# One fused attention and MLP kernel, the same operations in another order table

## The chip, the cores and the metric

The kernel runs on one core of one Trainium2 chip. The metric is the device time of one execution in microseconds (us), as the median of three runs. Five engines work side by side, each through a queue of its own, in order: TensorE (PE in the profile, PEld its weight loads), VectorE (DVE), ScalarE (ACT), GpSimd (POOL) and SyncE (SP). The last two also issue the DMAs: POOL the loads that cast from float32 to bfloat16, SP the stores and the DMA transposes.

## What is computed

Attention over a window of 128 keys and 4 sink keys, for 4 batches of 8 heads, 768 positions and 64 features; its output, 3072 rows of 512, goes through two matrix products with a squared ReLU between them.

```
scores = q @ k^T / sqrt(64);  keep = (pos_k < 4) | (0 <= pos_q - pos_k < 128)
a = softmax(where(keep, scores, -1e9));  x = a @ v            # 4 x 8 x 768 x 64
h = x.reshape(3072, 512) @ w_in                                # 512 x 2048
g = relu(h) ** 2
out = g @ w_out                                                # 2048 x 512, float32
```

## The kernel before

The work is cut into 996 operations, each one or a few instructions on one engine. For every batch: load q, k and v; bring q and k into the layout with the features on the partitions (by transposes on TensorE and copies out of PSUM for batches 0 and 1, lines 508, 193 and 195; by DMA transposes from SP, line 462, for batches 2 and 3); scores into `ps` (L614), the exponential on ScalarE into `expm` (L635); the mask either on VectorE (L647, one instruction for a tile) or on GpSimd (L219, two instructions for a tile); the product with v into `po` (L683); the division by the sum into `xn_sb` (L699, L700); the turn of `xn_sb` into `xT` (L732 on TensorE for batches 0 and 1, DMA transposes L714 for 2 and 3); the scores of the sink keys are `pk` (L573). Layer 1 is `pm` (L764 for batch 0, L892 later), its ReLU `r` (L776 and L967 on ScalarE, L778 and L969 on VectorE), its square `gT_sb` (L785 and L915 on ScalarE, L787 and L917 on VectorE). Layer 2 is `py` (L1239, L1100), gathered into `osb` by copies and additions and stored by L1282. From batch 1 on layer 1, and everywhere layer 2, is a fast product with seven instead of eight partial products; the sums that it needs are `wi`, `wt`, `xs` and `sg` on VectorE (L811, L1031, L1213). The layer-2 products of one batch and the layer-1 products of the next stand between the attention pieces, so that TensorE has work while the other engines prepare its operands.

Nothing in the program decides the order at run time: the table ORDER does, a list of the 996 operations. A letter behind a number picks the engine where more than one can do it (`a` ScalarE, `d` VectorE, `g` GpSimd; without one, the first of its list), and a number behind a plus sign picks which of two pools of PSUM banks gives the room. Each engine's instructions stand in its queue in that order:

```
for word in words:
    word, *chosen = word.split("+")
    n = int(word.rstrip("pdag"))
    o = self.ops[n]
    o.engine = names[word[-1]] if word[-1] in names else next(iter(o.engines))
    for s in o.takes:
        if len(s.pools) > 1:
            s.pool = s.pools[int(chosen.pop(0))]
        s.room = free[s.pool].pop(0)
    self.idle = DUMMIES.get(n, 0)
    o.run(o.engine)
```

PSUM is held in four rooms (two pools of two). An operation that takes a room waits until those that read its last content are done. DUMMIES names small matmuls in front of early operations, all among the first 86, that keep TensorE busy while it waits for the first loads.

Of the kernel before, what the change touches and what calls it, by code (L numbers as in the profile page):

```python
# [20 lines left out]
ORDER = """  # L21
994 0 1 2 7 8 9 10 11 12 13 14 15 16 17 18 995+0 3 5 19 20 21 6 79 22 23 24 25 55d 56d 57+0 58 59 60a 83+0 85 103+1
105 26 27 28 62d 61d 63+1 64 67d 68d 65a 69+0 70 71 72 66a 84+1 73a 74a 75+1 76 78 91+0 86 77a 93 80 113+1 87+0 92+1
89 94 95+0 97 115 88 90 96 98 114+1 99+0 101 117 100 104+0 102 4 29 106 30 107 81+1 31 82 156+0 109+1 116 118 162+0
108d 32 111 157 112 119+1 168+0 121 120 110 123+1 122 125 174+1 163 126 335 169 124a 171+0 131+0 128+1 33 208 34 164
133 170a 175 35 36 37 172 38 132 39 40 158 130a 129a 144+1 146 137+0 176 136+0 147d 145+1 138 140 139d 177+0 278 134+0
148 159+1 135 149d 141d 142+0 279 143 173a 41 178 150+1 282+0 42 151 179a 152+0 43 153a 280 160 154 44 165+0 155a 45
274 189+1 166 180+1 275 276 284 161a 127 285 190d 277 281 283 181 337 286 287 46 192+1 289 196+0 193 200+0 194 197
167a 47 195a 201 297 336 288 48 202 338 183+0 198a 199a 203a 212+0+0 49 290 182 292 184d 215 294 230+0+1 291 299 50
293 298 191 213 231 186+1 204+0 233 295 185 187d 51 52 300 206a 301+0 251+1 303 248+0 205 188a 207a 232d 249a 304 253  # L30
252a 339 316 305d 296 302 219+1+0 216 317 308 53 318 209 306 307d 220 54 222 214 210+0 250a 319 309 234 448 237+0+1
310 311 211 235+0 238 217+0 240 218 236 223 340 466 239d 320+0 449 312 241d 221 450 322 256+0+0 451 259 257 313 452
453 323 454 455 314 341 321 456 242+0 244+0 457 324 458 224+1 327 459 325 460 461 243 471 225 326 226+0 254+1 246 245a
329 228 330 229a 247a 227 331 315 347+1 343 363+1 342 349 469 345 328 332 365 348 364 344 346 255 351 350 333 367
263+1+1 462 366 353 369d 352 479 354 260d 264 368 370 355d 379+0 470 467 266 358 356 468 395+0 258 359 463 371 372
357a 374 360d 361 381 265 373a 380 376 267d 375 474 383 261+0 382 362a 377 397 396 268+0 477 384 262 385 399 386 270+0
475 398 269 387d 272 273 378a 400 473 401 464 478 465 402 271a 489+0+0 390 411 492 490 388 392 403d 391 334 406 404
407 482+0+0 412 393 432+0 483 433 389 476 434 416+1 472 413 394 408 409 436 414 405 417 418 435 534+0 410a 438 420 692
419 536 437 530 422 439 415 421 693 423 532 440 537 485 443 441 491 424 694 427 533 538 444 695 442a 429 696 697 493
531 445 425 539 494+0 428 446 426a 535 495 480+0 540 430 698 447a 498+1+0 481 699 484 486 544 700 499 543 487+0 549  # L40
501 431 488 568 545 713 572+0 505+0+0 569 574 500d 546 541 508 506 542 573 521+0+0 547 710 714 701 579 522 570 575 576
514+1+0 509d 571 496 702 577 703 524 715 578 507 510+0 548 515 523d 582 580 550 723 497 581 583 502 517 585 553+0 551
503+0 511 704 711 516 554 584 587 588 592+0 589 504 594 525 526+0 705 590 518d 555 527 593 717 556 557 591 519+0 712
716 596 520 558 559d 598 552 749+0+0 706 707 595 722 560 561 563 512 750 752 597 599 513 600 562 742+0+0 753d 565d 528
564 603 743 601 751 602 566 604 745 586 726+0+0 529 720 605d 721 608+0 727 609 606 610 660+1 661 662 611 729 624 644+0
718 663 626 612 730 719 724+0 613 625 567 614 725 615 754+0 616 607 728 664 665 645 617 666 646 755 667 618a 648 647
668 619 744 620 649 627 650d 651 731+0 746 669 621 671 672 708 622 676+0 670a 677 673 732 652 674 747+0 623 678 655
653 679 680 656 681 675a 748 657 658 628+1 629 682 630 659 733+1+0 683 774 632 631 734 778+0 684 654a 775 634 685 735
633 779 635 686a 780 636 776 687 688 736 777 709 756 781 689d 690 758+0+1 759 637 782 761 639 640 638a 737 738+0 783
641d 739 642 691a 785 765+0+0 762d 784 760 643 797+0 768 766 793 787 757 799 794 788 769 789 763+0 795 740 767d 790d  # L50
741 791 764 798 786 831 800 801 836+1 837 834 802 832 792 838d 852+0 833 854d 853 840 804 796 855 856 803 839 806 858d
770+0 771 807 857 812 835 813 859 842 808 841 843 772 805 814 810 816+1 860 773 863 861 817 865 844d 864 847 845 809
823 866 818d 846a 868 848 867a 872+0 869 849 874 871 920+0 862 819 850 820 922 873 904+1 870 815 921 905 875 906d 876
877 923 851a 924 821 936 822d 878 879 907 925 811 926 908 880 825 883 827 937 927 881 826 938 882 828 910 885 824 829
884 909 886 888+1 911 928d 889 887 940+0 890 892 942 891 929 893 939 931 894d 932 912 915 930a 895 933 896 934 943 913
916 897 899 914a 944 900 945 935 917 830 946 901 898 941 959+0 902 918 949 947 919a 903 955 957 950 951 956 953 948
961 960 974 962 966 952d 976 978+1 963 975 958 979 964 981+1 965d 954 980 968 967 977 982 983d 970 969 985 984 986 989
972 987 971 988 990 973 993 992 991
"""
DUMMIES = {  # L60
    995: 29, 58: 8, 63: 10, 64: 4, 83: 3, 91: 3, 97: 3,
# [1345 lines left out]
```

## Time and profile before

| what | value |
|---|---|
| median of three runs | 210.26 us (210.16 to 212.4) |
| the profiled execution, its own time | 209.92 us |
| its span, first to last instruction | 208.1 us |
| granted TensorE clock | 1.000 |
| TensorE busy | 198.7 us, 95% of the span |
| VectorE busy | 175.4 us, 84% |
| ScalarE busy | 140.0 us, 67% |
| GpSimd busy | 94.0 us, 45% |
| moved by DMA | 26.12 MB |

The span leaves out 1.82 us of the execution's own time, which lie before the first and behind the last instruction. Matmuls overlap, so that a matmul's duration in the profile is longer than the distance from it to the next; eight matmuls of 256 columns with their weight loads advance TensorE by 0.87 us.

### The profile page before, as it was taken

What the parts mean: (1) busy time and instruction counts of PE and PEld (TensorE: products, weight loads), DVE (VectorE), ACT (ScalarE), POOL (GpSimd) and SP (SyncE); (2) the same over time, 40 slices, a digit from 0 to 9 for tenths busy, and PEclk for the clock granted to TensorE, in tenths of its full rate; (3) what the DMA queues carried; (4) which work ended last, traced back from release to release, by engine and by line L of the source; (5) the groups of instructions that cost most, each with busy time, mean ns of one, the idle gap of its engine ahead of it and who ended that gap; (6) DMA issues with size and microseconds to landing.
All of it is one profiled execution on the core that took longest, in us unless ns stands there. A gap on an engine that the chain in (4) does not pass through costs nothing.

```text
span 208.1 us, 6073 instructions
## 1 busy us (share of the span) xinstructions
PE 198.7 (95%) x2524; PEld 178.7 (86%) x2524; DVE 175.4 (84%) x343; ACT 140.0 (67%) x218; POOL 94.0 (45%) x134
## 2 busy tenths in 40 slices
PE   7779989999999999999999999999999999999993
PEld 7548878998888889889878989998889999999892
DVE  5844647988998899999997988999999998999753
ACT  2686679865895579999977459789892176475010
POOL 7999983597289907319629937100230000000000
PEclk9999999999999999999999999999999999999999
DMA  5999999999999999999999998902022230110205
GB/s 169 278 187 206 174 197 215 166 150 142 158 68 146 147 198 154 166 142 82 143 133 214 110 149 161 186 3 50 3 50 104 30 126 3 41 60 3 101 3 202
DMA packets 93995, 26.12 MB, mean 125 GB/s; under 512 B 86800, under 2 KB 91408, under 8 KB 93968
## 3 DMA queue, kind: packets, MB, share of 16 engines
q0 software_dynamic: 69248, 12.59, 87.1%
q1 hardware_dynamic: 24536, 13.01, 28.7%
q8 instruction: 20, 0.33, 0.6%
q10 hardware_dynamic: 184, 0.14, 0.2%
q14 instruction: 7, 0.06, 0.1%
HBM read 27.30 MB, written 6.29 MB: 161 GB/s over the span
## 4 chain that ended last, share of the span: by engine, by line
PE 70%; DMA 13%; POOL 5%; ACT 4%; DVE 3%; SPq 2%; issue 1%; ACTq 0%; DVEq 0%; POOLq 0%
PE py L1239 31%; PE pm L892 23%; DMA w_out_sb<-in_moe_w_out_dram 6%; PE po L683 5%; PE ps L614 5%; DMA qn<-in_q_dram 4%; DMA qr<-in_q_dram 3%; PE pm L764 2%; POOL expm L219 2%; PE py L1100 2%; SPq L352 2%; ACT expm L635 1%; PE pt L508 1%; ACT gT_sb L915 1%; POOL qn L373 1%
## 5 line engine op out<-in xcount | busy, mean ns | idle before, releaser
L635 ACT ACTIVATE expm<-ps 128x1024 bf16<-128x1024 f32 (+1 forms) x48 | 43.8, 956 | 4.3 <-PE ps L614 3.9
L219 POOL TENSOR_SCALAR_AFFINE_SELECT expm<-expm 128x512 bf16<-128x512 bf16 x30 | 20.9, 726 | 42.2 <-ACT expm L635 33.6
L942 DVE CUSTOM_DVE_ANT_0 r<-pm,t 128x512 bf16<-128x512 f32 x54 | 36.1, 684 | 2.3 <-ACT t L193 1.4
L1239 PEld LDWEIGHTS <-gT_sb 128*128 128x128 bf16 x352 | 33.0, 98 | 4.6 <-issue 1.1
L892 PEld LDWEIGHTS <-w_in_sb 128*128 128x128 bf16 x384 | 32.7, 114 | 1.0 <-issue 0.5
L193 ACT ACTIVATE t<-pm 128x512 f32<-128x512 f32 x42 | 24.9, 599 | 12.3 <-PE pm L892 11.1
L193 ACT ACTIVATE osb<-py 128x256 f32<-128x256 f32 x36 | 13.6, 384 | 26.1 <-PE py L1239 23.7
L1239 PEld LDWEIGHTS <-sg 128*128 128x128 bf16 x264 | 24.9, 98 | 3.4 <-issue 0.8
L892 PEld LDWEIGHTS <-wi 128*128 128x128 bf16 x288 | 24.8, 114 | 0.8 <-issue 0.5
L1239 PE MATMUL py<-wt,sg 128*128 128x256 bf16 x176 | 22.8, 273 | 0.0
L1239 PE MATMUL py<-w_out_sb,gT_sb 128*128 128x256 bf16 x176 | 22.7, 273 | 0.0
L1239 PE MATMUL py<-wt,gT_sb 128*128 128x256 bf16 x176 | 22.7, 273 | 0.0
L764 PE MATMUL pm<-xT,w_in_sb 128*128 128x256 bf16 x192 | 22.5, 273 | 0.1
L915 ACT ACTIVATE gT_sb<-r 128x1024 bf16<-128x1024 bf16 x21 | 22.1, 1058 | 0.7 <-DVE r L942 0.7
L892 PE MATMUL pm<-xs,w_in_sb 128*128 128x256 bf16 (+1 forms) x192 | 21.3, 246 | 0.0
L892 PE MATMUL pm<-xs,wi 128*128 128x256 bf16 (+1 forms) x192 | 21.2, 246 | 0.0
L764 PEld LDWEIGHTS <-w_in_sb 128*128 128x128 bf16 x192 | 20.6, 114 | 0.6 <-issue 0.2
L683 PE MATMUL po<-v,expm 128*128 128x65 bf16 x352 | 18.0, 193 | 0.4 <-ACT expm L635 0.3
L700 DVE TENSOR_TENSOR xn_sb<-po,rc 128x512 bf16<-128x512 f32 (+1 forms) x28 | 17.2, 615 | 1.0
L683 PEld LDWEIGHTS <-expm 128*128 128x128 bf16 x352 | 16.8, 97 | 1.4 <-issue 0.6
L614 PE MATMUL ps<-qkT 64*128 64x128 bf16 (+1 forms) x256 | 14.5, 238 | 1.4 <-ACT qkT L193 1.1
L1253 DVE TENSOR_TENSOR osb<-py,osb 128x256 f32<-128x256 f32 x33 | 13.3, 418 | 2.8 <-PE py L1239 1.9
(107 smaller groups left out, 372.1 us busy)
## 6 DMA issues: line engine op xcount, KB each, us to landing
out_dram<-osb SPq DMA_DIRECT2D x11, 512.0 KB, 3.1
v<-in_v_dram POOLq DMA_DIRECT2D x24, 128.0 KB, 7.0
qn<-in_k_dram POOLq DMA_DIRECT2D x20, 128.0 KB, 6.6
qn<-in_q_dram POOLq DMA_DIRECT2D x20, 128.0 KB, 6.9
w_in_sb<-in_moe_w_in_dram POOLq DMA_DIRECT2D x4, 512.0 KB, 10.1
w_out_sb<-in_moe_w_out_dram POOLq DMA_DIRECT2D x4, 512.0 KB, 9.8
qr<-in_k_dram SPq DMA_DIRECT2D x4, 256.0 KB, 5.3
qr<-in_q_dram SPq DMA_DIRECT2D x4, 256.0 KB, 4.8
```

The lines of the kernel that those rows point to most:

```text
L193: return nc.scalar.activation(out=dst, in_=src, func=AF.Copy)
L219: nc.gpsimd.affine_select(out=e_tile, in_=e_tile, compare_op=ALU.is_ge, fill=fill, base=i - 1, pattern=[[0, n], [1 if i else -1, 128]], ch ...
L614: nc.tensor.matmul(ps[:, h2, o:o + w], lhsT=qkT_sb[r, m, 1, c, :], rhs=qkT_sb[r, m, 0, qb:qb + w // 128, :], start=(i == 0 and not biased) ...
L635: nc.scalar.activation(out=x[:, :, o:512], in_=bank_t["s", b, s, m][:, :, o:512], func=AF.Exp, scale=scale)
L683: touch(("po", b, s, m0), e, nc.tensor.matmul(pv[:, i, h2, :], lhsT=lhsT, rhs=rhs, start=(n_ == 0), stop=(n_ == len(mms) - 1)), j)
L700: touch(("po", b, s, m0), e, nc.vector.tensor_tensor(out=xn_sb[:, 2 * s:2 * s + 2, 128 * (m0 + j0):128 * (m0 + j0 + nj)].rearrange("p i (j ...
L764: nc.tensor.matmul(pm[:, i, :], lhsT=w_in_sb[:, fb // 4, kb, fb % 4:512:4], rhs=xT[:, c0 // 256:(c0 + cw) // 256, kb, :], start=(kb == 0), ...
L892: touch(tag, e, nc.tensor.matmul(y[:, bk, i, :], lhsT=weights(name, f0 + i, a), rhs=rhs[:, a, :], start=fresh and i == 0 and a == 0, stop= ...
L915: nc.scalar.activation(out=d, in_=x, func=AF.Square)
L942: touch(tag, e, nc.vector._custom_dve(TENSOR_ADD_SAT, out=d.rearrange("p n c -> p (n c)"), in0=T["y"][:, 1].rearrange("p n c -> p (n c)"), ...
L1239: touch((b, u), e, nc.tensor.matmul(region(name), lhsT=x[:, i, :], rhs=w_[:, i, :], start=first and i == 0, stop=i == HB - 1, skip_group_c ...
L1253: ins = nc.vector.tensor_tensor(out=d, in0=region(of), in1=d, op=ALU.add)
```

## The change

ORDER is replaced behind its first 86 entries. The operations, their number, the data that they move and DUMMIES stay. What changes is the order on every queue, the engine of 64 pieces that ScalarE or VectorE can do and of 11 masks that VectorE or GpSimd can do, and the choice of some PSUM rooms.

```
 105 26 27 28 62d 61d 63+1 64 67d 68d 65a 69+0 70 71 72 66a 84+1 73a 74a 75+1 76 78 91+0 86 77a 93 80 113+1 87+0 92+1
-89 94 95+0 97 115 88 90 96 98 114+1 99+0 101 117 100 104+0 102 4 29 106 30 107 81+1 31 82 156+0 109+1 116 118 162+0
-108d 32 111 157 112 119+1 168+0 121 120 110 123+1 122 125 174+1 163 126 335 169 124a 171+0 131+0 128+1 33 208 34 164
...
+89 94 95+0 97 115 88 90 96 98 114+1 99+0 101 117 100 104+0 102 4 29 106 81+1 107 156+0 82 157d 158 109+1 116 162+1
+119+0 118 108d 163 121 111 30 110 112 168+0 120 31 122 32 123+1 124a 125 33 208 174+1 126 171+0 164a 175 131+0 169d
...
```

Three places, as the engines' queues read before and now.

GpSimd, the loads of batches 0 and 1 (`qn` and `v` are loads of q, k and v, `w_out_sb` the second weight matrix, `expm` the masks of batch 0, `mask` a constant tile that batch 1 reads); a minus is what stood there before, a plus what stands there now:

```order
 L373 DMA qn<-in_q_dram 128x8x64
-L219 AFFINE_SELECT expm<-expm 128x4x128 x2
+L219 AFFINE_SELECT expm<-expm 128x4x128 x6
 L373 DMA qn<-in_q_dram 128x8x64
-L382 DMA v_181<-in_v_dram 128x8x64
-L219 AFFINE_SELECT expm<-expm 128x4x128 x4
-L382 DMA v_181<-in_v_dram 128x8x64
+L382 DMA v_181<-in_v_dram 128x8x64 x2
 L317 DMA w_out_sb<-in_moe_w_out_dram 128x2048
 L555 TENSOR_TENSOR vs_175<-vs_in,head_rows 32x130 x4
-L317 DMA w_out_sb<-in_moe_w_out_dram 128x2048 x3
```

Two masks now stand ahead of one load of q and one of v. Further on, the three instructions that write `mask` have moved from behind a load of batch 1 to between the second and the third load of `w_out_sb`.

VectorE at the same time, before:

```order
L195 COPY xT_184<-px 128x512 x2
L647 TENSOR_TENSOR expm<-expm,tri 128x1024
L699 RECIPROCAL rc<-po 128x4
L700 TENSOR_TENSOR xn_sb<-po,rc 128x2x128
L699 RECIPROCAL rc<-po 128x4
```

and now:

```order
L195 COPY xT_184<-px 128x512 x2
L778 TENSOR_SCALAR r<-pm 128x1024
L787 TENSOR_TENSOR gT_sb<-r 128x4x256
L647 TENSOR_TENSOR expm<-expm,tri 128x1024
L699 RECIPROCAL rc<-po 128x4
L700 TENSOR_TENSOR xn_sb<-po,rc 128x2x128
```

A ReLU, which ScalarE did before, and its square stand ahead of VectorE's own mask; on TensorE the product that reads this mask has gone behind the two that read GpSimd's.

SP, from the DMA transposes of batch 2's attention output (`xT_184`) to those of batch 3's q and k (`qkT_180`), before:

```order
L714 DMA_TRANSPOSE xT_184<-xn_sb 128x4x128 x3
L1282 DMA out_dram<-osb 128x1024
L714 DMA_TRANSPOSE xT_184<-xn_sb 128x4x128
L462 DMA_TRANSPOSE qkT_180<-qn 128x4x128 x4
L1282 DMA out_dram<-osb 128x2x512
L714 DMA_TRANSPOSE xT_185<-xn_sb 128x4x128 x4
```

and now:

```order
L714 DMA_TRANSPOSE xT_184<-xn_sb 128x4x128 x4
L462 DMA_TRANSPOSE qkT_180<-qn 128x4x128 x4
L1282 DMA out_dram<-osb 128x2x512
L1282 DMA out_dram<-osb 128x1024
L714 DMA_TRANSPOSE xT_185<-xn_sb 128x4x128 x4
```

A store has moved behind the four transposes of q and k. Within the four the first of k (operation 718) now stands ahead of both of q (720, 721), where it was the third; the other of k (719) is last in both.

More of the change, by code (lines that the diff above doesn't have):

```diff
@@ L23 @@
 105 26 27 28 62d 61d 63+1 64 67d 68d 65a 69+0 70 71 72 66a 84+1 73a 74a 75+1 76 78 91+0 86 77a 93 80 113+1 87+0 92+1
-89 94 95+0 97 115 88 90 96 98 114+1 99+0 101 117 100 104+0 102 4 29 106 30 107 81+1 31 82 156+0 109+1 116 118 162+0
-108d 32 111 157 112 119+1 168+0 121 120 110 123+1 122 125 174+1 163 126 335 169 124a 171+0 131+0 128+1 33 208 34 164
-133 170a 175 35 36 37 172 38 132 39 40 158 130a 129a 144+1 146 137+0 176 136+0 147d 145+1 138 140 139d 177+0 278 134+0
-148 159+1 135 149d 141d 142+0 279 143 173a 41 178 150+1 282+0 42 151 179a 152+0 43 153a 280 160 154 44 165+0 155a 45
@@ L28 @@
[L28 to L57, printed above, removed]
@@ L58 @@
-972 987 971 988 990 973 993 992 991
+89 94 95+0 97 115 88 90 96 98 114+1 99+0 101 117 100 104+0 102 4 29 106 81+1 107 156+0 82 157d 158 109+1 116 162+1
+119+0 118 108d 163 121 111 30 110 112 168+0 120 31 122 32 123+1 124a 125 33 208 174+1 126 171+0 164a 175 131+0 169d
+172 128+1 34 335 127 133 35 132a 36 130a 129 144+1 37 170 38 146 136+0 176 137+0 39 138 140 177+0 40 145+0 139d 134+0
+41 135 42 43 44 45 148 147d 159+0 141d 278 142+0 336 149d 150+0 143 151 160 282+0 279 152+0 154 284d 280 46 274 155a
@@ new lines @@
+153a 161 173a 275 178 165+1 179a 189+1 180+0 276 338 181d 47 281 283 285 166 289 190 286 48 192+1 49 167 196+0 287
+200+0 193 277 290 50 194 197 288 297 201 51 299 195a 292 298 183+0 202a 291 198a 203a 199a 212+0+0 213 52 184d 293 300
+215 230+0+1 182 53 186+1 295 294d 231 204+1 191 233 54 341 301+0 187 206a 232 185a 296 248+0 251+0 205 234 302 249a
+303d 304 207a 305 253 250 448 219+0+1 214 222 252 188 209 308 449 316 220 337 306 210+0 307 211 237+0+1 240 311 216
+238 309 310 313 235+0 221 223 317 236 312 314 450 451 217+0 218 320+0 256+0+0 322 254+1 259 255 318 241d 257 323 319
@@ new lines @@
+321 239d 224+1 452 225 453 242+0 243 339 324 325 454 326 226+1 228 229a 470 455 244+0 246 247a 227a 342 327 456 258d
+330 469 245a 329 363+1 331 343 340 457 466 347+1 344 328 364 349 365 332d 348 345 333 350 351 353d 367 366 263+1+1 467
+346 352 458 354 459 369 368 478 355d 460 461 468 356 264 370 266 371 474 379+0 395+0 372 357a 358 462 397d 359 373a
+381 380 463 396 360d 374 375 361 376 315 476 260 464 265 479 261+0 382 465 362a 383 399 385 267 377 262 268+0 384 386
+473 398 269 387d 270+0 272 273 400 471 378a 401 271a 402 411 489+0+0 390 492 388 391 403d 414 404 490 406 412 392 407
@@ new lines @@
+475 482+0+0 472 393 389 692 432+0 483 394 434 433 413 408 409 416+1 436 418 405 417 534+0 435 437 693 438 410a 419 493
+420 439 530 422 440 532 421 415 423 536 424 443 441 537 427 477 694 485 425 444 491 484 428 538 426a 445 334 429 695
+710 531 539 430 494+0 540 535 446 495 533 480+0 431a 498+1+0 543 486 544 713 447 696 481 501 487+0 442a 488 568 545
+546 499 505+0+0 508 697 698 712 541 506 711 572+0 569 496 574 699 570 573 521+0+0 547 542 524 575 549 550 723 514+1+0
+700 579 576d 701 507 502d 577 497 509 515 522 578 702 553+0 571 516d 551 510+0 587 581 554 714 580 588 548 500d 517
@@ new lines @@
+523d 703 589 716 704 705 511 717 583 503+0 525 560 518 582 519+0 504 584 706 715 526+0 585 552 555d 520 512 592+0 527
+513 556 594d 590 528 529 561 557 749+0+0 593 596 718 595 750 720 558 598 559d 707 721 562 752 597 599 600d 753 742+0+0
+563 591 603 719 564 743 745 601 626 566 565 602a 604 751 726+0+0 605d 624 722 608+0 727 606 609 660+1 610 661 662 611
+729 612 613 663 614 724+0 644+0 615 708 725 730 744 754+0 616 625 664 607 746 619 627 645 646 617 665 666 618a 728 567
+667 648 647 620 668 650 649 755 621 671 731+0 651 669 672 670a 709 622 732 652 673 676+0 678 674 623 628+1 655 677
@@ new lines @@
+675a 747+0 653 679 629 656 657 748 680 630 682 658 681 733+1+0 734 683 774 632 659 684 736 775 778+0 631 685 634 687
+633 654a 780 737 689 635 776 735 688 636 690 779 758+0+1 761 691 759 781 686 639 782 637 785 777 738+1 739 640 638a
+783 797+0 641 784 586 642 787 788 643a 765+0+0 793 740 756 789 794 799 768 798 741 795 760 790 757 786 800 791 792 762
+766 763+0 804 831 801 852+0 832 853 834 812 854 833 836+1 837 769 767 835 838 856 802 858 840 842 855 764 839 770+0
+857 805 841 843 771 814 844 796 816+1 803 772 859 845 847 860 818d 807 806 773 861 848 863 864 808 846 849d 819 865
@@ new lines @@
+813 866 850 867a 872+0 810 809d 868 904+1 869 817 820d 870 920+0 906 862a 922 851 873 921 924 815 874 923 821 876 925
+878 875 905 822d 926 936 908 877 826 825 907 927 828 879 938 880 871 928d 823 883 937 929 827 881 882a 829 931 885 824
+932 884 909 888+1 889 910d 886 890 940+0 930 891 887a 830 933d 892 893 911 894 895 934 942 943 912 896 899 915 935a
+944 811 917 913 897 900 914a 916 945 901 941 946 947 939 950 918 919 902 898a 959+0 952 903 949 974 955 957 951 975
+953 956 978+1 961 958 962 948 954 960 979 976 963 964 966 965d 977 968 980d 981+0 970 967 983d 972 982 969 985 984
@@ L59 @@
+971d 986 989 973 987 988 990 993 992 991
 """
```

## The prediction

> **What bounds the kernel now.** I read the page's first lines, then the busy time in four stretches of the span, then the chain that ended last, and then the timelines of TensorE, GpSimd and SP where TensorE has gaps.
>
> ```profile
> span 208.1 us, 6073 instructions
> PE 198.7 (95%) x2524; PEld 178.7 (86%) x2524; DVE 175.4 (84%) x343; ACT 140.0 (67%) x218; POOL 94.0 (45%) x134
> 0.00:16.40 16.40, 12.45 (x166) 9.44 (x166) 10.38 (x30) 10.23 (x16) 13.99 (x28) 1.00 1.22 211
> 16.40:49.00 32.60, 31.02 (x393) 28.89 (x392) 22.40 (x41) 23.39 (x31) 25.41 (x37) 1.00 1.83 181
> 49.00:204.50 155.50, 155.22 (x1968) 140.32 (x1967) 142.28 (x273) 106.34 (x173) 54.60 (x71) 1.00 1.04 104
> 204.50:208.10 3.60, 0.05 (x1) 0.00 (x0) 0.37 (x2) 0.00 (x0) 0.00 (x0) 1.00 0.47 163
> ```
>
> The stretches list the busy time of PE, PEld, DVE, ACT and POOL, then the clock. TensorE is the bound, at full clock. Its missing 9.4 us lie as follows: 3.95 before 16.4 us, where the table has not changed; 3.55 behind 204.5 us, the last copies and stores; 32.60 - 31.02 = 1.58 in between up to 49 us; and 155.50 - 155.22 = 0.28 in the 155 us after that. The operations stay the same, so a table can win what is idle, and no more: 1.58 + 0.28 = 1.86 us, 0.9%. It can lose without such a limit. By a measurement that tells 1% from no change (2.1 us here), even the whole of it is not a clear win.
>
> The gaps before 49 us, on TensorE:
>
> ```profile
> 23.80 0.50 PE L732 MATMUL px<-ident,xn_sb 128*128 128x128 bf16 x6
> 24.70 0.29 PE L732 MATMUL px<-ident,xn_sb 128*128 128x128 bf16 x2 [0.40 <-DVE xn_sb L700]
> 29.65 0.40 PE L614 MATMUL ps<-qkT 64*128 64x128 bf16 x6 [0.28 <-ACT r L776]
> 30.63 0.84 PE L614 MATMUL ps<-qkT 64*128 64x128 bf16 x18 [0.58 <-ACT qkT L193]
> 47.33 0.55 PE L508 MATMUL pt<-ident,qn 128*128 128x128 bf16 x7
> 48.06 0.90 PE L508 MATMUL pt<-ident,qn 128*128 128x128 bf16 x13 [0.18 <-DMA qn<-in_q_dram]
> ```
>
> Three waits, for a norm, for a room that a ReLU holds, and for a copy; and a fourth, for a load of batch 1's q. The chain that ended last says what that load hangs on:
>
> ```profile
> 26.51 12.56 DMA w_out_sb<-in_moe_w_out_dram
> 39.07 0.28 issue
> 39.36 8.66 DMA qn<-in_q_dram
> 48.06 0.47 PE pt L508 x5
> ```
>
> The reader is to see that the load is issued 0.29 us after the last of `w_out_sb` has landed, and that TensorE starts 0.04 us after the load itself has.
>
> **The change, part by part.** *Up to 49 us.* GpSimd's queue there:
>
> ```profile
> 16.80 1.23 POOL L219 TENSOR_SCALAR_AFFINE_SELECT expm<-expm 128x512 bf16<-128x512 bf16 x2
> 17.97 0.89 POOL L373 DMA_DIRECT2D qn<-in_q_dram  x1
> 18.85 0.88 POOL L382 DMA_DIRECT2D v<-in_v_dram  x1
> 19.73 2.39 POOL L219 TENSOR_SCALAR_AFFINE_SELECT expm<-expm 128x512 bf16<-128x512 bf16 x4
> 27.66 2.65 POOL L373 DMA_DIRECT2D qn<-in_k_dram  x3 [0.62 <-DMA qn<-in_q_dram]
> 32.25 0.87 POOL L373 DMA_DIRECT2D qn<-in_q_dram  x1 [0.81 <-DMA w_out_sb<-in_moe_w_out_dram]
> 34.48 0.87 POOL L373 DMA_DIRECT2D qn<-in_q_dram  x1 [1.36 <-DMA w_out_sb<-in_moe_w_out_dram]
> 36.92 0.87 POOL L373 DMA_DIRECT2D qn<-in_q_dram  x1 [1.56 <-DMA w_out_sb<-in_moe_w_out_dram]
> 39.36 0.88 POOL L373 DMA_DIRECT2D qn<-in_q_dram  x1 [1.56 <-DMA w_out_sb<-in_moe_w_out_dram]
> 41.23 1.01 POOL L259 COPY mask<-tri 128x128 bf16<-128x128 bf16 x1
> 42.18 0.40 POOL L260 COPY mask<-tri 128x256 bf16<-128x256 bf16 x1
> 42.63 0.30 POOL L261 MEMSET mask<- 4x256 bf16 x1
> ```
>
> The two masks (2.39) move ahead of two loads (0.89 + 0.88), so they end at about 18.0 + 2.4 = 20.4 instead of 22.1. The two products that read them follow at once on TensorE; the third product, whose mask now waits on VectorE behind a ReLU (1.23) and a square (0.69), comes last and is hidden by them. The norm that TensorE waits for at 24.70 is then ready 0.4 to 0.7 earlier. The waits at 29.65 and 30.63 are shortened too, since VectorE has taken two ReLUs off ScalarE there, but one copy that a score reads is still second in ScalarE's queue, so I leave half of their 0.86. TensorE comes to 48 us some 0.4 + 0.4 = 0.8 us earlier, between 0.4 and 1.3.
>
> There it meets the load. Does the load come earlier? It is gated by the last landing of `w_out_sb`. That transfer and the one before it are issued later now by the three instructions that write `mask`: 1.01 + 0.40 + 0.30 = 1.7 us. But the last of them takes 12.56 us from issue to landing, against 8.66 for the next load, so it stands in a backlog several us deep, and GpSimd's waits behind it, 0.62 + 0.81 + 1.36 + 1.56 + 1.56 = 5.9 us, take up the 1.7. The landing stays at 39.07 and the load at 48.02. What is won ahead of 48 us is lost in the wait; what is left is one group of four transposes of k (about 0.2 us, an estimate: the chain has 0.47 for five, the end of the pipeline included) that stood behind the load and now stands ahead of it. **-0.2 us**; bounds: -1.3 if the load came earlier by as much as TensorE, +1.7 if the backlog were gone and the 1.7 passed on.
>
> *From 49 us on.* TensorE has next to no gap here, so only new waits count. Groups of 0.87 us have changed places with score groups and products between which ScalarE must finish:
>
> ```profile
> 110.01 0.61 PE L614 MATMUL ps<-qkT 64*128 64x128 bf16 x12
> 108.02 1.02 ACT L635 ACTIVATE expm<-ps 128x1024 bf16<-128x1024 f32 x1 [0.24 <-PE ps L614]
> ```
>
> The scores at 110.01 take the room that the exponential from 108.02 to 109.04 frees, with 0.97 us to spare; one layer-2 group fewer stands between them now (0.87), and the exponential ahead of it on ScalarE is the same. That leaves 0.1 us, less than a queue's usual jitter; a place like it is where batch 2's layer 1 begins to mix with batch 3's scores, near 135 us. I take 0.15 us for each of the two and nothing for the others, whose producers move with them: **+0.3 us**; bounds -0.28 (all gaps gone) and +1.5 (ten such places).
>
> *Who does the pieces.* Eight masks go from VectorE to GpSimd, three come back; of the pieces that ScalarE and VectorE share, 34 go to VectorE and 30 leave it. By kind that is one square, one ReLU of 1024 columns and copies that even out within 0.1 us.
>
> ```profile
> L917 DVE TENSOR_TENSOR gT_sb<-r 128x1024 bf16<-128x1024 bf16 x15 | 10.2, 685 | 0.1
> L778 DVE TENSOR_SCALAR r<-pm 128x1024 bf16<-128x1024 f32 x3 | 3.7, 1225 | 0.9 <-PE pm L764 0.9
> L647 DVE TENSOR_TENSOR expm<-expm,tri x17: 679/686/1118, 18.0 to 155.7; 128x1024 bf16<-128x1024 bf16 x17
> L219 POOL TENSOR_SCALAR_AFFINE_SELECT expm<-expm x30: 624/636/1084, 16.8 to 154.2; 128x512 bf16<-128x512 bf16 x30
> 107.90 3.91 POOL L219 TENSOR_SCALAR_AFFINE_SELECT expm<-expm 128x512 bf16<-128x512 bf16 x4 [5.50 <-issue]
> 108.12 1.12 DVE L647 TENSOR_TENSOR expm<-expm,tri 128x1024 bf16<-128x1024 bf16 x1
> ```
>
> VectorE: 0.69 + 1.23 + 0.1 - 5 x 0.69 = -1.4 us of 175; GpSimd: five masks of 2 x 0.64 = +6.4 of 94. Neither total decides; the place of a mask does. On GpSimd it takes 1.27 us instead of 0.69, and where both engines work at once (107.90 and 108.12) each is stretched: the mask to 3.91 / 2 = 1.95, VectorE's instruction from 0.69 to 1.12. Through those four masks TensorE lost nothing that the stretches show. I take **0** for it, with up to 2.4 us in the rivals; what hides it is the layer-2 work on TensorE between a mask and its product, and without that cover each of the eight would cost 0.6 to 1.3 us.
>
> The Trainium skill, "SBUF — State Buffer", section "Who interferes with whom", says that a VectorE instruction with two SBUF inputs and a GpSimd instruction that reads SBUF cannot run together: the one that comes second stands still until the first has ended. The rows at 108 us agree in kind, with 0.43 us of stretch. By that rule the net ten further GpSimd instructions could hold VectorE for 10 x 0.43 = 4.3 us (an estimate from the row), which speaks against the change.
>
> *SP near 125 us.*
>
> ```profile
> 122.43 0.53 SPq L1282 DMA_DIRECT2D out_dram<-osb  x1
> 123.01 1.46 SPq L714 DMA_TRANSPOSE xT<-xn_sb  x1
> 124.56 6.71 SPq L462 DMA_TRANSPOSE qkT<-qn  x4
> 130.28 0.40 PE L573 MATMUL pk<-qkT,kblk 128*32 128x512 bf16 x4 [0.16 <-ACT expm L635]
> ```
>
> The sink scores at 130.28 read the transposes of q. A transpose of k now goes ahead of these: 6.71 / 4 = 1.7 us, less the store's 0.53. Against that, batch 2's products that these transposes wait behind stand up to 0.9 us earlier. I take **0**; bounds 0 and +1.2. Behind a late transpose wait the sink scores, and in SP's queue two stores that nobody needs soon.
>
> *The end.* TensorE's last four groups and VectorE's last four operations stand in the same order: **0**.
>
> Sum: -0.2 + 0.3 = +0.1 us on the profiled 209.92 (208.1 of span and 1.82 around it), 210.0. The median of the runs is 0.34 above that execution; so 210.26 + 0.1, and I say **210.4 us**.
>
> **The rivals.** *A, faster:* the load moves with TensorE and the waits before 49 us go (the load's landing in its row is all that stands against it): -1.58 - 0.28, 208.4 us. *B, slower:* masks on GpSimd arrive late. Of the eight, three meet VectorE and are read with 0.5 us to spare: 3 x (1.95 - 0.69 - 0.5) = 2.3 us, 212.7; it decides from three on, since two give 1.5 (211.9). For it speak the row at 107.90 and VectorE's 142.28 busy of 155.50, which leave it no time to catch up; against it, VectorE's smaller total. The skill's rule named above would work in this way. *C, slower:* loads and transposes of batch 3 come late; on GpSimd two masks now stand ahead of two loads of v and one more ahead of loads of q, and the 1.2 us on SP comes on top of 0.64 x 2 on GpSimd: +2.5 at most, +1.5 likely, 211.9. *D:* the early waits are new ones of the same length, 210.6, inside the forecast.
>
> **How the numbers follow.** Forecast with D 0.60 (209.3 to 211.5 by its bounds), A 0.12, B 0.18, C 0.10. Faster by over 1% needs nearly all that is idle: half of A, 0.06. Slower by over 1%: B and half of C, 0.23. The rest, 0.71, is within 1%. The range goes from 208.8, which leaves out half of A, to 213.0, which takes in B with three masks and leaves out four.
>
> **What would show it.** Right: TensorE's busy time about 198.7 again; a wait for `qn` near 48 us longer than 0.18, with the last landing of `w_out_sb` at 39 us; gaps at 24.7 and 30.6 smaller; the stretch from 49 us on within 0.5 us of 155.50. Wrong: a landing of that load before 47 or after 49 us (A, or the upper bound); waits of `po` for GpSimd's `expm`, with masks of 1.9 us (B); a wait of `pk` or `ps` for a DMA between 120 and 135 us (C).

## The result: 0.4% slower, and the profile after

| | before | the change |
|---|---|---|
| median of 20 runs | 210.50 us (209.81 to 212.4) | 211.69 us (210.63 to 212.49) |
| the ratio of the times | 1 | 1.0041, interval 1.0021 to 1.0060 |
| the profiled execution | 209.92 us, span 208.1 | 212.38 us, span 210.7 |

Every ratio is taken against runs of the kernel before that were made along with it, without the few executions that lie over 1.5% above the fastest of their kernel. The change costs 0.4 to 1.3 us by the interval of its ratio, 0.86 in the middle; the two medians are 1.19 us apart. Within 1% was what I forecast, and 211.69 us lies in the range. The table below says, though, that two larger numbers of opposite sign have met in it.

The page's first lines after the change:

```profile
span 210.7 us, 6074 instructions
PE 199.8 (95%) x2524; PEld 178.8 (85%) x2524; DVE 178.3 (85%) x342; ACT 138.5 (66%) x214; POOL 101.6 (48%) x144
```

TensorE's share is the same. The busy time in stretches (PE, PEld, DVE, ACT, POOL, then clock), first of before, from 49 us on, and then of the change:

```profile
49.00:110.00 61.00, 60.87 (x792) 53.45 (x791) 57.23 (x109) 49.73 (x82) 36.27 (x46) 1.00 1.85 141
110.00:125.00 15.00, 15.00 (x246) 13.38 (x246) 12.46 (x27) 9.52 (x16) 10.95 (x16) 1.00 1.71 158
```

```profile
0.00:16.40 16.40, 12.59 (x158) 9.89 (x158) 9.93 (x28) 9.54 (x15) 14.04 (x28) 1.00 1.21 204
16.40:49.00 32.60, 31.11 (x396) 28.76 (x393) 25.73 (x47) 19.89 (x26) 25.19 (x37) 1.00 1.83 183
49.00:110.00 61.00, 61.00 (x809) 53.42 (x806) 57.38 (x110) 51.15 (x85) 39.21 (x49) 1.00 1.73 144
110.00:125.00 15.00, 13.61 (x210) 11.61 (x209) 14.23 (x26) 6.75 (x10) 9.41 (x11) 1.00 1.59 125
```

TensorE had no idle time between 110 and 125 us before and has 1.39 us there now, while VectorE, which had 2.5 us to spare, has 0.8. The rest of TensorE's loss shows only against its work. I compare the time between two points behind which the same groups of matmuls lie in both traces (the start of the next group, from the timelines):

| TensorE, us | before | the change |
|---|---|---|
| start of the span to point 1 (first layer-1 products of batch 0) | 18.77 | 19.59 |
| point 1 to 2 (a group of layer 2 of batch 1) | 91.79 | 91.01 |
| point 2 to 3 (a group of layer 1 or 2, all of batch 2's attention behind it) | 11.92 | 14.03 |
| point 3 to 4 (2.8 us before TensorE's end) | 79.27 | 79.21 |

Point 1 lies behind the 86 entries that are the same; its 0.8 us is a difference between two executions, not between tables (ten of the twelve kernels below, which share these 86 entries, came there between 18.50 and 19.55 us). So the new table wins 0.8 us up to 110 us and loses 2.1 in the next 12.

TensorE at the place of the gain, where before had waits at 24.70 and 48.06:

```profile
24.54 0.61 PE L732 MATMUL px<-ident,xn_sb 128*128 128x128 bf16 x8
25.70 3.69 PE L764 MATMUL pm<-xT,w_in_sb 128*128 128x256 bf16 x32 [0.55 <-DMA w_in_sb<-in_moe_w_in_dram]
30.55 0.40 PE L614 MATMUL ps<-qkT 64*128 64x128 bf16 x6 [0.28 <-ACT r L776]
31.53 0.62 PE L614 MATMUL ps<-qkT 64*128 64x128 bf16 x12 [0.58 <-ACT qkT L193]
48.45 1.06 PE L508 MATMUL pt<-ident,qn 128*128 128x128 bf16 x16
```

The wait for the norm is gone (the eight turns of `px` are one group now) and so is the one for the load of q; the two at 30.55 and 31.53 are exactly as long as before. But a new one of 0.55 us, for a load of the weights `w_in_sb`, stands right behind the turns. It says nothing of the order: in eight of eleven traces of the kernels below TensorE waits for these weights too, for 0.33 to 0.93 us, also where the old table stands there, and before's execution was free of it. And TensorE at the place of the loss, with its waits from 110 to 125 us:

```profile
116.20 0.24 PE L683 MATMUL po<-v,expm 128*128 128x65 bf16 x2 [0.95 <-DVE expm L647]
```

```profile
PE po L683 <- DVE expm L647: 1.0, 1, 1.0
PE ps L614 <- DVE xn_sb L700: 0.3, 1, 0.3
```

A product waits for a mask on VectorE, and 6 us later scores wait for a division on VectorE (it frees their room). VectorE and GpSimd there:

```profile
110.31 1.12 DVE L1213 TENSOR_TENSOR sg<-gT_sb,sg 128x1024 bf16<-128x1024 bf16 x1
111.35 1.11 DVE L647 TENSOR_TENSOR expm<-expm,tri 128x1024 bf16<-128x1024 bf16 x1
112.39 1.11 DVE L1213 TENSOR_TENSOR sg<-sg,gT_sb 128x1024 bf16<-128x1024 bf16 x1
...
114.29 2.90 DVE L647 TENSOR_TENSOR expm<-expm,tri 128x1024 bf16<-128x1024 bf16 x2
117.11 0.71 DVE L854 TENSOR_TENSOR xs<-xd,xs 128x256 bf16<-128x256 bf16 x1
```

```profile
110.83 1.77 POOL L416 DMA_DIRECT2D v<-in_v_dram  x2
112.59 1.77 POOL L404 DMA_DIRECT2D qn<-in_k_dram  x2
114.34 3.34 POOL L219 TENSOR_SCALAR_AFFINE_SELECT expm<-expm 128x512 bf16<-128x512 bf16 x4
```

Two masks that take 0.69 each alone take 2.90 beside four selects of GpSimd. The product waits for the first of them (operation 500). This mask was the 532nd entry of the old table, and VectorE did it at 106.26 us, ahead of GpSimd's selects; it is the 574th of the new one. Its row before:

```profile
106.26 0.68 DVE L647 TENSOR_TENSOR expm<-expm,tri 128x1024 bf16<-128x1024 bf16 x1
```

### The profile page after: what moved, and what is told of

The parts are those of the page before. It is cut to its first block, busy times and chain, and to the rows that moved or that the text cites. A ratio compares the mean times of both kernels' runs of the same rounds, so it can differ in the third digit from the quotient of the medians.

```text
span 210.7 us, 6074 instructions
## 1 busy us (share of the span) xinstructions
PE 199.8 (95%) x2524; PEld 178.8 (85%) x2524; DVE 178.3 (85%) x342; ACT 138.5 (66%) x214; POOL 101.6 (48%) x144
## 4 chain that ended last, share of the span: by engine, by line
PE 77%; DVE 7%; DMA 6%; POOL 5%; ACT 2%; issue 1%; POOLq 0%; ACTq 0%
PE py L1239 29%; PE pm L892 26%; PE pm L764 8%; DMA w_in_sb<-in_moe_w_in_dram 6%; PE ps L614 5%; PE po L683 4%; DVE expm L647 2%; POOL v L382 2%; PE py L1100 2%; DVE xn_sb L700 1%; PE pt L508 1%; DVE sg L1213 1%; POOL w_in_sb L309 1%; PE px L732 1%; POOL vs L555 1%
## 5 line engine op out<-in xcount | busy, mean ns | idle before, releaser
L219 POOL TENSOR_SCALAR_AFFINE_SELECT expm<-expm 128x512 bf16<-128x512 bf16 x40 | 28.0, 735 | 41.7 <-ACT expm L635 38.6
L193 ACT ACTIVATE t<-pm 128x512 f32<-128x512 f32 x45 | 26.1, 599 | 12.8 <-PE pm L892 12.0
L892 PEld LDWEIGHTS <-w_in_sb 128*128 128x128 bf16 x384 | 32.2, 114 | 1.1 <-issue 0.7
L892 PEld LDWEIGHTS <-wi 128*128 128x128 bf16 x288 | 24.7, 114 | 0.7 <-issue 0.3
L915 ACT ACTIVATE gT_sb<-r 128x1024 bf16<-128x1024 bf16 x22 | 23.2, 1059 | 2.7 <-PE py L1239 1.6
L193 ACT ACTIVATE osb<-py 128x256 f32<-128x256 f32 x31 | 12.0, 386 | 19.6 <-PE py L1239 19.5
L764 PEld LDWEIGHTS <-w_in_sb 128*128 128x128 bf16 x192 | 20.4, 114 | 1.3 <-DMA w_in_sb<-in_moe_w_in_dram 0.7
L892 PE MATMUL pm<-xs,w_in_sb 128*128 128x256 bf16 (+1 forms) x192 | 20.8, 246 | 0.0
L892 PE MATMUL pm<-xs,wi 128*128 128x256 bf16 (+1 forms) x192 | 20.6, 246 | 0.0
```

Of the source, the lines that this page charges most:

```text
L193: return nc.scalar.activation(out=dst, in_=src, func=AF.Copy)
L219: nc.gpsimd.affine_select(out=e_tile, in_=e_tile, compare_op=ALU.is_ge, fill=fill, base=i - 1, pattern=[[0, n], [1 if i else -1, 128]], ch ...
L764: nc.tensor.matmul(pm[:, i, :], lhsT=w_in_sb[:, fb // 4, kb, fb % 4:512:4], rhs=xT[:, c0 // 256:(c0 + cw) // 256, kb, :], start=(kb == 0), ...
L892: touch(tag, e, nc.tensor.matmul(y[:, bk, i, :], lhsT=weights(name, f0 + i, a), rhs=rhs[:, a, :], start=fresh and i == 0 and a == 0, stop= ...
L915: nc.scalar.activation(out=d, in_=x, func=AF.Square)
```

## The experiments

Four theories. *Theory 1:* mask 500 stands too late in VectorE's queue. *Theory 2:* VectorE and GpSimd, which hold each other up, are together short of time in this stretch, whichever mask is first. *Theory 3:* the loss is made elsewhere. *Theory 4:* SP's new order costs time near 130 us. In the diffs below, words of the table stand with their neighbours.

**Which half.** The tables can be joined at entry 485 (about 95 us): the first 485 entries of one, then the rest in the order of the other.

```
second kernel:  new[:485] + the rest in the old order
third kernel:   old[:485] + the rest in the new order
```

> The new table up to its entry 485 (about 95 us), the old one behind it. Theories 1 and 2, the loss lies behind 105 us: 0.998 to 1.001 of the kernel before, stretch 16.4 to 49 us as with the new table. Theory 3, the loss lies in the first half: 1.004.

> The old table up to its entry 485 (about 95 us), the new one behind it. Theories 1 and 2: the wait of po near 115 us is there, 1.004 to 1.009 of the kernel before. Theory 3: 1.000 if the loss lies in the first half.

Measured: the second 0.9959 (0.9938 to 0.9981) of before, the third 1.0142 (1.0108 to 1.0175). The third one's trace has the same wait at the same place:

```profile
116.45 0.24 PE L683 MATMUL po<-v,expm 128*128 128x65 bf16 x2 [0.95 <-DVE expm L647]
```

Theory 3 falls: the first half of the new table is a gain, the second the whole loss. The third is slower than the 1.009 that I had allowed, and the halves, -0.41% and +1.42%, don't add up to the whole, +0.41%: some 1.3 us of the third kernel's loss are not in the change. Its trace has 14.02 us from point 2 to 3, as the change (14.03), and 92.35 from point 1 to 2, with 0.39 of it a wait for `w_in_sb`; where the rest comes from stays open (five runs). The gain was so much more than I had forecast that I ran the second kernel once more.

> The second kernel once more, beside the other two: 0.994 to 0.998 of the kernel before if the new table's first half is worth 0.4% whatever the landings of the loads; 1.000 if the first result was chance.

Measured: 0.9951 (0.9923 to 0.9980). This version, the new table up to 95 us and the old one behind it, is faster than both kernels, by 0.4 to 0.5% of before.

**Where the gain lies.** The same join at entry 211:

```
new[:211] + the rest in the old order
```

> The new table up to its entry 211 (about 47 us), the old one behind it. If the gain of the first half (0.4%) comes from the waits at 24.7 and 29.7 us alone: 0.997 to 0.998. If it comes from the order around the load of batch 1's q at 48 us and behind it: 0.999 to 1.000. If TensorE only meets the load again, as I forecast: 0.999 to 1.000 too, with a wait for qn near 48 us of 0.5 us or more.

Measured: 0.9978 (0.9953 to 1.0002). About half of the gain is there at 47 us, which speaks for the waits at 24.7; the interval doesn't exclude the other readings, but there was no wait for `qn` near 48 us. In its profiled execution, 1.6 us above the median of its runs, the old order loses time between points 2 and 3 too (13.37 us): layer 1 waits for a copy on ScalarE, and the copy for a DMA transpose of `xT`.

```profile
117.97 0.61 PE L892 MATMUL pm<-xd,w_in_sb 128*128 128x128 bf16 x8 [1.29 <-ACT xd L193]
```

The five other traces with the old order there (before, the second kernel twice, and two below that change one entry of it) all take 11.92 us, and the three with the new order and its engines 14.02 to 14.04, so this wait doesn't touch the comparison.

**Mask 500 first.**

```
-577 578 702 553+0 571 516d ... 580 588 548 500d 517 523d
+577 578 702 553+0 500d 571 516d ... 580 588 548 517 523d
```

> One VectorE mask of batch 2 (operation 500, read by product 503) moved ahead of a sum and a mask, as it stood in the old table. Theory 1, the late mask: the product finds its mask, the wait of 0.95 us ahead of po near 116 us is gone and no other of that length comes, so the time falls by about 1.0 us, to 0.999 to 1.002 of the kernel before. Theory 2, VectorE and GpSimd together are short of time there: the wait only goes to the next product that reads a mask (519 or 526), and the time stays at 1.003 to 1.005. Theory 3, the loss is made elsewhere (up to 49 us, or at the transposes): stays at 1.004 whatever that wait does.

Measured: 1.0047 (1.0025 to 1.0070), as the change. The product's wait is gone, and another has come, for an addition on VectorE that frees a room of `py`, behind the same masks. TensorE's waits between 110 and 122 us:

```profile
PE py L1239 <- DVE osb L1253: 0.7, 1, 0.7
PE ps L614 <- DVE xn_sb L700: 0.3, 1, 0.3
```

Points 2 to 3 take 13.62 us, so 0.4 of the 2.1 is back in this trace, though not in the runs. Theory 1 falls: the place of the mask decides only who waits.

**Masks 518 and 525 on VectorE** (the fourth kernel).

```
-503+0 525 560 518 582
+503+0 525d 560 518d 582
```

> The new table with masks 518 and 525 given to VectorE instead of GpSimd, at their places. Theory 2, the two engines hold each other up: VectorE's masks 500 and 523 go from 1.45 us each to 0.69, the four masks take 2.8 us on VectorE alone against 3.3 on both together, the wait of po for mask 500 falls from 0.95 to 0.3 or less, and the time by 0.3 to 0.8 us; theory 1, only the place of mask 500 counts and the stretch is small: its wait stays above 0.6, product 519 waits for masks 525 and 518 besides, and the time rises by up to 1 us.

Measured: 0.9982 (0.9961 to 1.0002), 1.2 us less than the change. VectorE in this kernel:

```profile
109.34 1.11 DVE L1213 TENSOR_TENSOR sg<-gT_sb,sg 128x1024 bf16<-128x1024 bf16 x1
110.37 0.68 DVE L647 TENSOR_TENSOR expm<-expm,tri 128x1024 bf16<-128x1024 bf16 x1
110.97 0.68 DVE L1213 TENSOR_TENSOR sg<-sg,gT_sb 128x1024 bf16<-128x1024 bf16 x1
...
112.44 1.28 DVE L647 TENSOR_TENSOR expm<-expm,tri 128x1024 bf16<-128x1024 bf16 x2
...
114.68 1.28 DVE L647 TENSOR_TENSOR expm<-expm,tri 128x1024 bf16<-128x1024 bf16 x2
```

Masks 500 and 523 take 1.28 instead of 2.90, and with 518 and 525 besides VectorE is through all four in 2.56: less time than it needed for two of them while GpSimd did the others. Points 2 to 3 take 12.30 us, against 14.03 and 11.92 of before, and no `po` waits for a mask. Theory 2 stands. From before to the change the number of masks that each engine has in this stretch stayed the same. The groups by shape between 106 and 118 us, of before, the change and this kernel:

```profile
L647 DVE TENSOR_TENSOR expm<-expm,tri 128x1024 bf16<-128x1024 bf16 x4 | 3.6, 900 | 0.0
L219 POOL TENSOR_SCALAR_AFFINE_SELECT expm<-expm 128x512 bf16<-128x512 bf16 x8 | 6.7, 873 | 5.9 <-issue 5.5 <-ACT expm L635 0.4
```

```profile
L647 DVE TENSOR_TENSOR expm<-expm,tri 128x1024 bf16<-128x1024 bf16 x4 | 4.8, 1215 | 0.0
L219 POOL TENSOR_SCALAR_AFFINE_SELECT expm<-expm 128x512 bf16<-128x512 bf16 x8 | 6.9, 907 | 9.9 <-ACT expm L635 9.9
```

```profile
L647 DVE TENSOR_TENSOR expm<-expm,tri 128x1024 bf16<-128x1024 bf16 x6 | 4.0, 696 | 0.0
L219 POOL TENSOR_SCALAR_AFFINE_SELECT expm<-expm 128x512 bf16<-128x512 bf16 x4 | 3.6, 926 | 9.1 <-ACT expm L635 9.1
```

Four tiles on VectorE and four (eight selects) on GpSimd, before as after. What the new order changed is when they meet: more of VectorE's lie beside the selects (mean 1215 ns instead of 900), and closer ahead of their products.

**One mask back.** Mask 518 is one of those that the change moved to GpSimd; 525 was there in both tables.

```
-525 560 518 582
+525 560 518d 582
```

> The new table with mask 518 alone back on VectorE, where the old table had it; 525 stays on GpSimd, as in both tables. If the one moved mask makes the loss: the wait of po near 115 us falls below 0.3 us and the time to 0.998 to 1.000 of the kernel before, as with both masks on VectorE. If it takes VectorE's masks 500 and 523 beside any GpSimd mask: half of it goes, the wait is 0.5 to 0.8 us, 1.000 to 1.003. If the selects of 518 only came behind the harm that those of 525 do: 1.004.

Measured: 1.0020 (0.9994 to 1.0046), about half way between the change and both masks back. How long the product waits here isn't known, so the time alone speaks: the middle case is the nearest, though the interval touches both neighbours.

**A GpSimd mask where VectorE does other work.** In the faster version, mask 518 to GpSimd:

```
-526+0 705 590 518d 555
+526+0 705 590 518 555
```

> The second kernel (new to 95 us, old behind) with mask 518 given to GpSimd, where it comes near 116 us beside VectorE's divisions and short sums and 1 us ahead of its product. Theory 2 in its narrow form, a GpSimd mask costs only where VectorE has long SBUF work at once and a product follows closely: the divisions keep their 0.69 us, no wait of po, 0.994 to 0.997 of the kernel before. In its broad form, every further mask on GpSimd costs: 0.2 to 0.3% more, 0.997 to 0.999. If the two loads of q behind it, 1.27 us later, are what counts: a longer wait of the sink scores near 129 us for their transposes, 0.997 or above.

Measured: 0.9973 (0.9951 to 0.9995). Points 2 to 3 take 11.92 us, exactly as without the move. GpSimd and VectorE there:

```profile
117.93 1.29 POOL L219 TENSOR_SCALAR_AFFINE_SELECT expm<-expm 128x512 bf16<-128x512 bf16 x2
```

```profile
117.92 0.80 DVE L854 TENSOR_TENSOR xs<-xd,xs 128x256 bf16<-128x256 bf16 x1
118.65 0.19 DVE L699 RECIPROCAL rc<-po 128x8 f32<-128x8 f32 x1
118.88 0.69 DVE L700 TENSOR_TENSOR xn_sb<-po,rc 128x512 bf16<-128x512 f32 x1
```

The short sum `xs` beside the selects takes 0.80 (0.29 without them), the division, whose large input `po` lies in PSUM, its usual 0.69. The selects cover only half of this division; before's trace has one that lies beside them whole, and it is not longer either:

```profile
71.17 1.25 POOL L219 TENSOR_SCALAR_AFFINE_SELECT expm<-expm 128x512 bf16<-128x512 bf16 x2
71.28 0.69 DVE L700 TENSOR_TENSOR xn_sb<-po,rc 128x512 bf16<-128x512 f32 x1
```

Where the product is 1 us away, that costs TensorE nothing: the narrow form of theory 2, by the trace. The ratio alone would fit both forms. The sink scores wait 0.50 us for their transposes, within what the two traces without the move show (0.59 and 0.20).

**All eleven masks on their old engines**, in the new order:

```
-232 ... 260 ... 258d ... 267 ... 509 ... 502d ... 516d ... 518 ... 753 ... 762 ... 767
+232d ... 260d ... 258 ... 267d ... 509d ... 502 ... 516 ... 518d ... 753d ... 762d ... 767d
```

> The new table's order with all eleven masks on the engines of the old table (eight from GpSimd to VectorE, three the other way). Theory 2, GpSimd's masks beside VectorE's cost the time: 509 and 518 leave GpSimd near 109 and 116 us but 502 and 516 come, so one tile's worth of selects is taken from the crowd where the fourth kernel took two; the wait ahead of po near 115 us halves, 1.000 to 1.003. Rival, the order alone makes the loss, whoever does the masks: 1.004 or above.

Measured: 1.0110 (1.0073 to 1.0147), worse than the change and outside what theory 2 gave; by its number the rival that stood beside it, that the order alone makes the loss, came true. Some of the loss is at the same place (points 2 to 3 take 13.40 us). GpSimd still has four tiles in this stretch, two of them others than in the change, and beside two of the selects a sum on VectorE takes 2.22 us instead of 0.69:

```profile
112.20 2.22 DVE L1213 TENSOR_TENSOR sg<-sg,gT_sb 128x1024 bf16<-128x1024 bf16 x1 [0.24 <-PE py L1239]
112.27 1.24 POOL L219 TENSOR_SCALAR_AFFINE_SELECT expm<-expm 128x512 bf16<-128x512 bf16 x2
```

Some is at a new place:

```profile
85.40 0.22 PE L683 MATMUL po<-v,expm 128*128 128x65 bf16 x2 [0.47 <-DVE rc L699]
```

Points 1 to 2 take 92.40 us, 1.4 more than with the change; this wait and one of 0.21 behind it are half of that. So it seems, from this one trace, that the moved masks were part of the gain in the first half. My expectation had looked at the second half alone. Order and engine can't be told apart by this run: it shows that the old engines don't repair the new order.

**SP's order.** The transposes of q ahead of that of k again (the fifth kernel):

```
-593 596 718 595 750 720 752 597 ... 707 721 562
+593 596 595 750 720 752 597 ... 707 721 718 562
```

> The new table with the DMA transposes of q (720, 721) ahead of that of k (718) again. Theory 4, the order on SP costs time behind the late masks: the sink scores find their q, their wait of 0.34 us near 132 us goes, 1.001 to 1.003 of the kernel before. Rival: the transposes are late as a whole, because SP starts them only behind those of the attention output, and one more or less ahead of q changes that wait by up to 0.3 us but not the time, 1.004.

Measured: 1.0051 (1.0026 to 1.0075), no difference from the change. And in the faster version, the store behind the transposes:

```
-745 586 726+0+0 529 720 ... 730 719 724+0
+745 726+0+0 529 720 ... 730 719 586 724+0
```

> The new table up to its entry 485, the old one behind it, and the store of an output tile (586) behind the transposes of batch 3's q and k instead of ahead of the last one of batch 2. Theory 4, SP's queue is the bound near 130 us: the transposes come 0.54 us earlier, the wait of the sink scores falls from 0.76 to 0.2, time 0.992 to 0.995 of the kernel before. Rival: they wait for data, not for SP's queue, 0.996 as without the move.

Measured: 0.9960 (0.9937 to 0.9983), as without the move, although the wait for the transposes is gone. The sink scores without the move, and with it:

```profile
129.62 0.40 PE L573 MATMUL pk<-qkT,kblk 128*32 128x512 bf16 x4 [0.59 <-DMA qkT<-qn]
```

```profile
129.74 0.40 PE L573 MATMUL pk<-qkT,kblk 128*32 128x512 bf16 x4
```

The wait is gone, as theory 4 has it, but it isn't shown that the store made it: the second trace of the version without the move has 0.20 us there, so it varies by itself. Half a microsecond is 0.25% of the time, and the two intervals don't separate that from nothing. Whether the store is worth its move stays open; the new SP order is not where the change lost.

**A repair that failed.** The change with 518 and 525 on VectorE, q's transposes first, and a sum and a copy behind VectorE's last divisions:

```
-715 526+0 585 552 555d 520 512 592+0 527 513
+715 526+0 585 520 512 592+0 527 552 555d 513
```

> The new table with masks 525 and 518 on VectorE, the transposes of q ahead of that of k (718), and one sum and one copy (552, 555) behind the last two divisions of batch 2 on VectorE. Theory 2: beside the wait of po near 115 us, that of the scores near 120 us (0.39 us in the fourth kernel) goes too, 0.994 to 0.997 of the kernel before. Rival: the scores wait for the division's product and not for VectorE's queue, 0.998 as the fourth kernel.

Measured: 1.0011 (0.9980 to 1.0042), where the two masks alone gave 0.9982; the intervals overlap. The scores no longer wait, but layer 2 does, since the copy that I had put back frees its room:

```profile
120.59 1.03 PE L1239 MATMUL py<-wt,sg 128*128 128x256 bf16 x8 [1.62 <-DVE osb L195]
```

## Right and wrong, step by step

**What bounds the kernel: right.** TensorE is busy 199.8 us; the loss is waits of TensorE, and so is about half of the gain. The rest is not: "a table can win what is idle, and no more" is too strict, as the part from 49 us on shows.

**Up to 49 us, forecast -0.2: wrong in size.** The step that failed is "There it meets the load". I took the landing of one execution, 48.02 us, for a fixed point. The third kernel has the old table there, and its TensorE went through the same transposes without a wait:

```profile
47.71 1.28 PE L508 MATMUL pt<-ident,qn 128*128 128x128 bf16 x20
```

The load had landed at 46.55 us there; in the change it landed at 48.21 and in the ten others with the new table there between 46.74 and 48.29. What made it late before was the load itself: 8.66 us from issue to landing, against 6.89 to 7.67 in these twelve traces. GpSimd's waits absorbed a part of the 1.7 us, not all: `w_out_sb`'s last landing was at 39.07 before and 39.38 with the old table in the third kernel, at 40.26 in the change and at 39.43 to 40.97 in the others. So two signs that I had named, that landing at 39 us and a longer wait for `qn`, did not come.

The norm's wait went, as forecast (0.4 to 0.7): up to the transposes of q and k at 28 us TensorE gains 0.53 to 0.66 from point 1 on in the three versions of the new table that don't wait for `w_in_sb`. In the change that wait took all of it. The half that I took off the waits of 0.28 and 0.58 did not come.

From the layer-2 group ahead of the transposes near 46 us to the layer-1 group near 54, the same groups of matmuls took TensorE 8.36 us before, 8.01 in the third kernel, which has the same table, and 7.80 in the change and the second kernel: 0.35 of before's was that one load, 0.21 is the new order's.

**From 49 us on, forecast +0.3 for two new waits: wrong in place.** Neither the scores near 110 us nor layer 1 near 135 us waits in the change, and no row stood behind the 0.15 us apiece. From the layer-1 group near 54 us to point 2 TensorE took 56.84 us in the two traces with the old table and 56.52 to 56.54 in the nine with the new one and its engines: 0.30 won where before has 0.13 idle from 49 to 110 us (61.00 - 60.87). A busy TensorE can still advance a little faster in another order; what makes it, the rows don't say. All in all the new order's 0.53 + 0.21 + 0.30 = 1.0 us agrees with the second kernel's runs, -0.4 to -0.5% or -0.9 to -1.0 us, where I had about 0; it lies within the bound of -1.3, and its sign is the one I gave to the part before 49 us.

**Who does the pieces, forecast 0: the term that failed.** The sentence is "Through those four masks TensorE lost nothing that the stretches show". That was true of the old order, where eight selects and four masks of VectorE share the same 12 us at no cost, and I carried it over to an order in which they meet closer to their products. It cost 2.1 us. VectorE's busy time, which my count of pieces lets fall by 1.4 us, rose by 2.9 (175.4 to 178.3). *Rival B*, with a chance of 0.18, had the stretching and the sort of place, but the wrong engine: it named waits for GpSimd's masks, and what came is a wait for VectorE's. That its price (2.3) is near is luck, for it counts masks newly on GpSimd, and there are eight selects in this stretch before and after. The Trainium skill's rule ("SBUF — State Buffer", section "Who interferes with whom") was the one that spoke against the change, and the trace agrees with its direction: the VectorE instructions that lie beside selects between 110 and 118 us lose 2.4 us together (one of 1.12 and two of 2.90 in sum, against 0.69 each, and 0.71 against 0.28); two more of 1.11, which lose 0.8, lie beside DMA issues alone. The same section says that a VectorE instruction with at most one input in SBUF, outside its two-port modes, doesn't contend; the two divisions beside selects, at 0.69, agree.

**SP, forecast 0: right**, as far as the fifth kernel's interval tells. **The end, forecast 0:** the order there gave none; the span's tail is 0.45 us longer in this one execution.

**Rival A**, the whole of the idle time won: by the second kernel as much as half of it was to be had, in the first half alone. **Rival C**, batch 3's transposes late: not in the change.

**The sum:** I wrote -0.2 + 0.3 + 0; the tables give -0.8 to -1.0 and +2.1 in the traces, +1.1 to +1.3, and the runs +0.86 (0.44 to 1.26). That 210.4 comes within 1.3 us of the measured time is luck: two terms that I had both near 0 have opposite signs.

## What to carry to other kernels

Read how long an instruction takes beside what the *other* engine does, and carry no duration and no cover from one order to another: it is where masks meet, not how many each engine has, that cost 2.1 us here. Before a wait's end is taken as fixed, ask whether it is a transfer's landing; those moved by 1.7 us between executions. And where a whole table is exchanged, cut it: half of it may be a gain (0.9955 on average here) that the other half hides.

## What the runs showed of the hardware

For these masks two engines at once were slower than one alone: four took VectorE 2.56 us, while two on VectorE beside two on GpSimd took 2.90 and 3.34, in the change and again in the fifth kernel. GpSimd's selects are stretched too: a mean of 907 ns there, 636 ns in the middle of all of before's.

Not settled: in the change VectorE's instructions at 111.35 and 112.39 take 1.11 us while GpSimd's rows show only DMA issues; in the fourth kernel the same two take 0.68 beside the same DMA issues. The two kernels differ on GpSimd only in the selects that wait behind these issues. Whether selects that are waiting hold VectorE, or the spans on GpSimd are shown too late, no run here tells.
